# Diagonal tiles of a causal mask packed by 64 keys, masks as products, and a hinted last branch, in an attention kernel bound by its exponentials

**Chip, cores, metric.** One core of one Trainium2 chip. The metric is the time of one execution in device microseconds (us), median of several runs. A program on one core gives one time per run, and every comparison is made with runs of the kernel before on the same chip.

## The reference, cut to what matters

Two independent attention blocks over 2048 rows of 1024, 32 heads of 32. A is plain attention; B has four segments of 512 rows, a causal mask inside each segment and a memory that is carried from one segment to the next.

```python
# A
qkv = (x @ wqkv) ...                            # 32 heads of 32
p = softmax(einsum('bhqd,bhkd->bhqk', q, k) * Dh ** -0.5)
a = einsum('bhqk,bhkd->bhqd', p, v) ... @ wo
# B, for each of 4 segments of L = 512
mask = (ar[:, None] < ar[None, :]) * -1e9       # keys after the query are dead
p = softmax(einsum('bhqd,bhkd->bhqk', qs, ks) * scale + mask)
a_dot = einsum('bhqk,bhkd->bhqd', p, vs)
o = g * a_mem + (1 - g) * a_dot                 # a_mem from the carried memory M, z
M, z = M + phi(ks)^T vs, z + sum(phi(ks))
```

## The kernel before

The kernel is written as many small processes (projections, score batches, exponentials, values, outputs) that ask for buffers and engines. A scheduler at build time, with a cost for every instruction, turns them into one fixed list of instructions for each engine. So every instruction's place in its engine's queue is decided before the kernel runs.

Scores lie transposed in PSUM: keys on the partitions, queries on the columns, one bank of 512 columns for each of four heads, two banks to a pair, three pairs. ScalarE reads a pair (1024 columns), takes the exponential and writes the tile PT in SBUF. TensorE then multiplies PT with the values, and VectorE (DVE) copies the sums out of PSUM; such a copy, which frees a bank, is called an evacuation below. One batch of A is 512 columns for four heads, so two exponentials. B's batches for one unit (a segment and four heads):

```python
def parts(self, u, k):          # (key tile, first query, width, column in the bank)
    ...                         # A cut
    return [[(0, 0, 512, 0)], [(1, 128, 384, 0), (3, 384, 128, 384)], [(2, 256, 256, 0)]][k]

def s_batch(self, u, k):        # cut: waits for data, slots of PT
    one = u[0] == "B" and k == 2
    npair = 1 if one else 2
    prs = yield acq(self.pairs, npair)          # PSUM pairs
    ...
    yield do("PE", lambda e: f(e, mms), r=keys, w=w, cost=N256, prio=0, mode=ROW)
    for x in range(npair):
        Q.spawn(self.exps(u, k, x, prs[x], slots[x], one))

def exps(self, u, k, x, pr, sl, one):           # cut
    yield do("ACT", lambda e: e.activation(ap, self.ps[:, pr[0]:pr[1] + 1, :], ACTF.Exp, scale=sc),
             r=[("ps", bk) for bk in pr], w=keys, cost=0.9035, prio=0)
    Q.give(self.pairs, [pr])
    if u[0] == "B":                             # which 128 x 128 pieces hold a diagonal
        if k == 2:
            ms = [(bass.AP(..., ap=[list(ap.ap[0]), [256, 4], [1, P]]), 4)]
        else:
            ms = [(ap[:, :, c:c + P], 2) for c in ((0,), (0, 384))[k]]
        for m, n in ms:
            yield do("POOL", lambda e, m=m, n=n: e.affine_select(m, m, pattern=[[0, n], [1, P]],
                     compare_op=ALU.is_ge, fill=0.0, base=0, channel_multiplier=-1), ...)
```

At the end a flag says whether a slow fallback program must run; every engine reads it and branches:

```python
def f(eng):
    self.R.play(eng, name)
    self.R.after(eng, self.flagop)
    v = eng.value_load(self.flag[0:1, 0:1])
    with eng.If(v != 0):
        ...                                     # the fallback: a large second program
    if name == "SP":
        self.R.drain(eng)                       # last transfers landed
```

## Time and profile before

| | before |
|---|---|
| time, median (3 runs) | 1113.5 us (1112.8 to 1113.8) |
| span of the profiled run | 1111.6 us |
| first exponential starts, last one ends | 10.37, 1100.42 us |
| spacing of two exponentials (end to end), median | 917 ns |
| stalls between exponentials after 60 us | 2.3 us |
| end of the span after the last output's issue | 5.14 us |

"Stalls" is a sum that is used all through: for each exponential the time from the end of the one before it to its own end, less 917 ns (490 for one of 512 columns), added up over all that start after 60 us. It says how much time ScalarE lost in the body, whatever it waited for.

ScalarE (ACT) is the bound; the prediction below shows the lines. Its waits, in this view "engine, tile, line, what it waited for: us in total, times, longest":

```profile
ACT WoB L1002 <- PE ps L973: 7.3, 2, 6.6
ACT outsb L1202 <- PE ps L1197: 4.2, 3, 2.4
ACT PT L1002 <- PE ps L973: 2.5, 6, 0.7
```

The first row is the start of the program, the second its end. In between only the third is left: 2.5 us for scores. The chain of work that ended last, as shares of the span:

```profile
ACT 90%; PE 6%; DVE 2%; DMA 1%; POOL 1%; issue 0%
```

### The profile page before, as it was taken

The page shows a single profiled execution, that of the slowest core. Times are in us where ns is not written, and L with a number is a line of the kernel's source. Part 1 is how long each engine was busy: PE and PEld are TensorE (multiplying, and loading weights), DVE is VectorE, ACT ScalarE, POOL GpSimd, SP SyncE. Part 2 cuts the span into 40 slices and gives each one's busy share as a digit, 9 for nine tenths or more (in the row PEclk, how much of TensorE's full clock was granted, in tenths as well). Part 3 has the DMA queues.
Part 4 walks back from the last instruction along what each step waited for, and adds up shares of the span by engine and source line. Part 5 has one row for each costly group of instructions (what it writes and reads, how often), then busy time and mean ns, then how long its engine had stood idle before and what let it go on. Part 6 is the DMA issues. An engine that isn't in the chain of part 4 may idle for free.

```text
span 1111.6 us, 52489 instructions
## 1 busy us (share of the span) xinstructions
PE 1043.3 (94%) x24445; PEld 539.9 (49%) x24445; DVE 725.5 (65%) x1472; ACT 1089.7 (98%) x1189; POOL 136.8 (12%) x287
## 2 busy tenths in 40 slices
PE   8999999999899999989999999899999999999997
PEld 4545445454454444444455454444544444455454
DVE  2356556545675888888676788777566677664333
ACT  6999999999999999999999999999999999999996
POOL 1011111100201212121110301201111111110000
PEclk9999999999999999999999999999999999999999
DMA  9543332252122222142212232241132222201111
GB/s 186 103 104 86 64 69 46 50 93 55 31 50 41 55 64 60 43 85 52 58 46 55 45 60 65 50 84 40 41 55 50 45 45 60 88 18 36 41 41 66
DMA packets 213763, 67.40 MB, mean 61 GB/s; under 512 B 202786, under 2 KB 210978, under 8 KB 213538
## 3 DMA queue, kind: packets, MB, share of 16 engines
q1 hardware_dynamic: 212066, 63.07, 26.7%
q8 instruction: 192, 3.15, 1.3%
q10 hardware_dynamic: 1472, 0.92, 0.3%
q14 instruction: 33, 0.27, 0.1%
HBM read 36.70 MB, written 8.39 MB: 41 GB/s over the span
## 4 chain that ended last, share of the span: by engine, by line
ACT 90%; PE 6%; DVE 2%; DMA 1%; POOL 1%; issue 0%
ACT PT L1002 89%; PE ps L688 2%; PE ps L1109 2%; PE ps L1197 1%; PE ps L973 1%; DMA PKt<-PH 1%; ACT OTA L1002 1%; POOL PT L1011 0%; DMA OTA<-in_A_x_dram 0%; ACT OTB L1002 0%; DVE xA L625 0%; DVE VT L693 0%; PE ps L1244 0%; DVE PH L831 0%; DVE PH L1039 0%
## 5 line engine op out<-in xcount | busy, mean ns | idle before, releaser
L1002 ACT ACTIVATE PT<-ps 128x1024 bf16<-128x1024 f32 x1164 | 1068.2, 1265 | 2.7 <-PE ps L973 2.5
L1109 PE MATMUL ps<-PT,ones 128*32 128x256 bf16 (+1 forms) x4784 | 283.6, 270 | 1.2 <-issue 1.2
L1109 PE MATMUL ps<-PT,VA 128*32 128x256 bf16 x4016 | 241.3, 274 | 6.1 <-ACT PT L1002 5.0
L973 PE MATMUL ps<-QA,KA 32*128 32x256 bf16 x4096 | 203.4, 273 | 30.7 <-ACT PT L1002 25.5
L688 PE MATMUL ps<-xB,WB 128*32 128x512 bf16 (+1 forms) x3332 | 205.3, 364 | 2.4 <-DVE OD L1150 0.7
L1011 POOL TENSOR_SCALAR_AFFINE_SELECT PT<-PT 128x256 bf16<-128x256 bf16 (+1 forms) x224 | 106.5, 483 | 814.2 <-ACT PT L1002 808.9
L688 PE MATMUL ps<-xA,WA 128*32 128x512 bf16 (+1 forms) x3476 | 205.2, 356 | 1.3 <-DVE xA L625 0.6
L973 PEld LDWEIGHTS ps<-QA,KA 32*128 32x128 bf16 x4096 | 61.1, 92 | 193.6 <-ACT PT L1002 184.9
L1109 PEld LDWEIGHTS ps<-PT,ones 128*32 128x32 bf16 x4784 | 128.0, 97 | 32.8 <-issue 16.5
L1109 PEld LDWEIGHTS ps<-PT,VA 128*32 128x32 bf16 x4016 | 107.1, 96 | 44.8 <-issue 17.1
L688 PEld LDWEIGHTS ps<-xA,WA 128*32 128x32 bf16 x3476 | 80.4, 96 | 78.6 <-issue 28.0
L1150 DVE COPY OD<-ps 128x512 f32<-128x512 f32 x127 | 86.7, 682 | 43.7 <-PE ps L1109 42.7
L688 PEld LDWEIGHTS ps<-xB,WB 128*32 128x32 bf16 x3332 | 77.3, 96 | 77.7 <-issue 31.3
L1202 DVE CAST outsb<-ps 128x512 bf16<-128x512 f32 x55 | 37.9, 689 | 73.7 <-PE ps L1197 73.7
L693 DVE CAST VT<-ps 128x512 bf16<-128x512 f32 x64 | 44.1, 689 | 61.4 <-PE ps L688 57.5
L693 DVE CAST KQB<-ps 128x512 bf16<-128x512 f32 x64 | 44.1, 689 | 60.2 <-PE ps L688 60.2
L1197 PE MATMUL ps<-WoB,OTB 128*32 128x512 bf16 (+1 forms) x1100 | 68.2, 366 | 0.6 <-DVE OD L1150 0.6
L1156 DVE STREAM_TRANSPOSE OD<-Rall 128x256 f32<-128x256 f32 x127 | 56.0, 441 | 3.2
L1153 DVE STREAM_TRANSPOSE Dt<-OD 128x256 f32<-128x256 f32 x127 | 55.5, 437 | 2.9
L1197 PE MATMUL ps<-xA,OTA 128*32 128x512 bf16 (+1 forms) x888 | 53.4, 367 | 0.3 <-DVE KQB L693 0.3
L1109 PE MATMUL ps<-PT,VB 128*32 128x256 bf16 (+1 forms) x768 | 43.7, 257 | 7.4 <-POOL PT L1011 3.1
L973 PE MATMUL ps<-KQB 32*128 32x128 bf16 (+3 forms) x512 | 43.3, 302 | 6.6 <-ACT PT L1002 4.9
(95 smaller groups left out, 690.5 us busy)
## 6 DMA issues: line engine op xcount, KB each, us to landing
WB<-in_B_wk_dram SPq DMA_DIRECT2D x32, 256.0 KB, 3.0
WB<-in_B_wq_dram SPq DMA_DIRECT2D x32, 256.0 KB, 3.0
WB<-in_B_wv_dram SPq DMA_DIRECT2D x32, 256.0 KB, 3.2
out_dram<-outsb SPq DMA_DIRECT2D x63, 128.0 KB, 1.9
WA<-in_A_wqkv_dram SPq DMA_DIRECT2D x23, 256.0 KB, 3.2
WoB<-in_B_wo_dram SPq DMA_DIRECT2D x1, 2048.0 KB, 9.8
xA<-in_A_wo_dram SPq DMA_DIRECT2D x1, 2048.0 KB, 8.3
OTA<-in_A_x_dram SPq DMA_DIRECT2D x2, 256.0 KB, 5.5
```

The costliest lines, as they stand in the source:

```text
L688: ins = e.matmul(self.ps[32 * c:32 * c + 32, bank, lo:hi], W[:, i, 32 * c:32 * c + 32], x(i)[:, lo:hi], start=st, stop=sp)
L693: return e.tensor_copy(dst, self.ps[:, bank, 0:n])
L973: ins = e.matmul(self.ps[:, bk, col:col + w], lhs(t, hs), rhs(q0, w, hs), start=True, stop=True)
L1002: yield do("ACT", lambda e: e.activation(ap, self.ps[:, pr[0]:pr[1] + 1, :], ACTF.Exp, scale=sc), r=[("ps", bk) for bk in pr], w=keys, cos ...
L1011: yield do("POOL", lambda e, m=m, n=n: e.affine_select(m, m, pattern=[[0, n], [1, P]], compare_op=ALU.is_ge, fill=0.0, base=0, channel_mul ...
L1109: ins = e.matmul(out, l, r, start=st, stop=sp)
L1150: yield do("DVE", lambda e: e.tensor_copy(OD[:, :], self.ps[:, OB, :]), r=[("ps", OB)], w=[("OD", x), ("Rb", x)], cost=dve(2 * QU), prio=0 ...
L1153: yield do("DVE", lambda e: e.transpose(Dt[:, :], Rb), r=[("Rb", x)], w=[("Dt", x)], cost=dve(QU), prio=self.par["fp"], hold=0.15)
L1156: yield do("DVE", lambda e: e.transpose(Rb.rearrange("p (a b) -> p a b", b=32), self.spread(Rc)), r=[("Rc", ui % 64)], w=[("Rb", x)], cost ...
L1197: ins = e.matmul(self.ps[32 * c:32 * c + 32, bank, lo:hi], lhs(j)[:, 32 * c:32 * c + 32], W(j)[:, lo:hi], start=st, stop=sp)
L1202: return f(self.outsb[ob][:, :], self.ps[:, bank, :])
```

## The change

Its intent: of each 128 x 128 diagonal tile the quarter that is dead as a whole (upper 64 keys, lower 64 queries) is no longer computed. Two live 64-wide pieces of two tiles share 64 columns, one in the lower and one in the upper 64 partitions, by adding two products in PSUM, one of them with keys of which half are zero (KZ). The values do the same with half-zeroed values (VZ) and half-zeroed ones. A unit then needs 512 + 512 + 128 columns per head in place of 512 + 512 + 256, and the third exponential has 512 columns in place of 1024. As one short exponential leaves an odd half batch, batches are now made of two items each, which take two pairs together. The masks become products with a 0/1 tile, on POOL for the first batch and on DVE for the others. The branch at the end gets a hint (`branch_hint`), and the last waits come in order of issue. mR, a scratch tile for reading B's memory, now lies in the bytes of ze, the scratch of VectorE's other work, and has to be acquired like it. Constants of the scheduler were searched anew.

```diff
+HINT = {"PE": 99999, "ACT": 300, "DVE": 700, "POOL": 999, "SP": 999}   # operations before the end
-    par = dict(b=(16, 12, 9), mem=-4, ..., rate=0.58, ahead=20, sl=4, pv=10, ob=4, ..., slk=0.12, ...)
+    par = dict(b=(16, 12, 9), mem=-2, ..., rate=0.6, ahead=28, sl=7, pv=18, ob=1, ..., slk=0.3, ..., mk=(0, 1, 1), mp=0, ...)
 ...
-                self.R.play(eng, name)
+                loc = self.R.play(eng, name, HINT[name])
-                with eng.If(v != 0):
+                eng.br_eq(v, 0, on_true=over, on_false=again).branch_hint(loc)
+                with self.nc.body(again, valid_engines=[eng.engine]):
 ...
+    def b_k(self, n):       # half of each key tile, on POOL
+        yield do("POOL", lambda e: e.tensor_copy(self.KZ[:, :, 0:H], src), ..., cost=0.45, prio=1)
+    def b_v(self, n):       # halves of the values, on POOL
+        for j in range(2):
+            yield do("POOL", lambda e, j=j: e.tensor_copy(self.VZ[H * j:H * j + H, j:4:2, :], ...), ..., cost=0.52, prio=1)
 ...
-        return [[(0, 0, 512, 0)], [(1, 128, 384, 0), (3, 384, 128, 384)], [(2, 256, 256, 0)]][k]
+        H = P // 2
+        return [[("lo", 0, H, 0), ("hi", 1, H, 0), (0, H, 512 - H, H)], [(1, P + H, 5 * H, 0), (2, 2 * P + H, 3 * H, 5 * H)],
+                [("lo", 2, H, 0), ("hi", 3, H, 0), (3, 3 * P + H, H, H)]][k]
 ...
-        prs = yield acq(self.pairs, npair)
+        prs = yield acq(self.pairs, 2)
+        if one[0]:          # a short item first: three pieces on TensorE
+            ops = [(st[0][:3], banks[0], 0.1, None), (st[1], banks[1], N256, None), (st[0][3:], banks[0], 0.1, True)]
 ...
-            yield do("ACT", lambda e: e.activation(ap, self.ps[:, pr[0]:pr[1] + 1, :], ACTF.Exp, scale=sc),
-                     ..., cost=0.9035, prio=0)
+            n = 2 * P if one else 512
+            to = bass.AP(..., ap=[list(ap.ap[0]), [n, 2], [1, n]])
+            yield do("ACT", lambda e: e.activation(to, self.ps[:, pr[0]:pr[1] + 1, 0:n], ACTF.Exp, scale=sc),
+                     ..., cost=0.483 if one else 0.91, prio=0)
 ...
-                yield do("POOL", lambda e, m=m, n=n: e.affine_select(m, m, ...))
+            if self.par["mk"][k]:
+                yield do("DVE", lambda e: e.tensor_tensor(d, d, m, ALU.mult), ..., cost=dve(sz), prio=self.par["mp"])
+            else:
+                yield do("POOL", lambda e: e.tensor_tensor(d, d, m, ALU.mult), ..., cost=0.25 + sz * 0.0014, prio=0)
```

## The prediction

> **What bounds the kernel now.** I read the page's head and busy times first, then the groups of ScalarE (ACT) with shapes kept apart, then ACT's own waits.
>
> ```profile
> span 1111.6 us, 52489 instructions
> PE 1043.3 (94%) x24445; PEld 539.9 (49%) x24445; DVE 725.5 (65%) x1472; ACT 1089.7 (98%) x1189; POOL 136.8 (12%) x287
> ...
> L1002 ACT ACTIVATE PT<-ps 128x1024 bf16<-128x1024 f32 x1164 | 1068.2, 1265 | 2.7 <-PE ps L973 2.5
> L1002 ACT ACTIVATE WoB<-ps 128x1024 bf16<-128x1024 f32 x8 | 7.6, 1025 | 7.3 <-PE ps L973 7.3
> L1002 ACT ACTIVATE OTA<-ps 128x1024 bf16<-128x1024 f32 x8 | 7.6, 1048 | 0.0
> L1002 ACT ACTIVATE OTB<-ps 128x1024 bf16<-128x1024 f32 x4 | 3.8, 1105 | 0.0
> L1202 ACT CAST outsb<-ps 128x512 bf16<-128x512 f32 x3 | 1.8, 585 | 4.2 <-PE ps L1197 4.2
> ```
>
> The four ACTIVATE rows are all exponentials of the program: 1164 + 8 + 8 + 4 = 1184, each 128x1024. Their busy time is 1087.2 us of a span of 1111.6; of the 1164 in steady state only 2.7 us of idle time stand before them. So ACT is the bound, with no gaps to fill, and one exponential costs its spacing, 1087.2 / 1184 = 0.918 us. The mean of 1265 ns in the first row is not that cost: consecutive instructions overlap. The chain of waits says the same: ACT has 90% of it, and its longest piece is 570.38 us for 622 exponentials, 0.917 each.
>
> The code accounts for 1184. A has 8 head groups x 8 query blocks x 8 key batches x 2 = 1024. B has 32 units (4 segments x 8 head groups), each with five: two for the first batch, two for the second, one for the third: 160. Of these 5120 columns, a causal mask over 512 keys in tiles of 128 needs 4 heads x (512+384+256+128) = 5120. All are used, but half of each diagonal tile is thrown away afterwards.
>
> Outside ACT's solid stretch are a start (first exponential at 10.37 us) and a tail. I read the tail from the timeline and from the DMA view over one late microsecond:
>
> ```profile
> 1105.80 0.58 ACT L1202 CAST outsb<-ps 128x512 bf16<-128x512 f32 x1 [0.71 <-PE ps L1197]
> 1105.83 0.15 DVE L1302 CAST flag<-ps 32x1 int32<-32x1 f32 x1 [0.41 <-PE ps L1197]
> 1106.41 0.36 ACTq L1204 DMA_DIRECT2D out_dram<-outsb  x1
> ```
> ```profile
> q8 instruction: 1, 0.02, 10.2%
> q14 instruction: 1, 0.01, 1.9%
> ```
>
> The first block is the last work of any engine; the last output transfer lands about 1.9 us after its issue (median of that row on the page), near 1108.3. The flag that decides the branch is there at 1106.0. Yet the span ends at 1111.6. The second block is the stretch 1108 to 1109 us: one instruction block on each of two fetch queues and nothing else. Fetches also occur between 1107 and 1108 and after 1110. So the end, some 3.3 us after the last output, is about instructions being fetched behind the branch over the large fallback program, not about data.
>
> [...] (1025 - 585) / 512 = 0.86 ns per column between an exponential of 1024 and a cast of 512. [...]
>
> **The change part by part.**
>
> *Packing.* Each diagonal tile of 128x128 has only three of its four 64x64 blocks alive. The change puts the two live 64-key triangular pieces of two tiles on the same columns, one on the upper and one on the lower 64 partitions, by accumulating two products with half-zeroed keys. A unit then has 512 + 512 + 128 columns per head instead of 512 + 512 + 256: four exponentials of 1024 and one of 512. The count stays 1184, but 32 of them are halved. With 0.427 each this is 32 x 0.427 = 13.7 us; with the trace's 0.86 ns it would be 14.1. I take 13.7. It lies fully on the path, since ACT has no idle time to give back.
>
> *Masks.* 224 selects on POOL go (192 x 449 ns and 32 x 683 ns, 107 us). In their place come 64 products of 256 elements on POOL (first batch), and 64 of 256 plus 32 of 512 on DVE. The nearest DVE rows are tensor_tensor of 256 with f32 inputs, 415 to 454 ns, and 512 columns at 689; that gives at most 64 x 0.45 + 32 x 0.69 = 51 us. [...] I estimate 40: DVE goes from 725 to some 765 us, 70% of a shorter span. POOL: 64 products at 0.7 (estimate, above the 522 ns of its 128-wide product) are 45 us, and 96 copies of half keys and half values at 0.45 are 43. With the rest that stays, POOL is near 120 us, 11%. Nothing of this is on the path.
>
> *TensorE.* The streamed columns do not change: scores 576 + 512 + 192 = 1280 per head and unit, as before; values 384 + 896 = 1280, as before. There are more and shorter matmuls: 32 instead of 16 for scores and 80 instead of 48 for values and sums, 48 x 32 = 1536 more. In the timeline four 256-wide ones start every 0.108 us, 0.027 per 64 columns. If a pack of 64 columns takes twice its share, about 20 packs a unit lose 0.027 x 20 x 32 = 17 us. TensorE's idle time is 68 us, and it also spends 18.7 us on fillers that multiply by zero. So it stays beside ACT, at 95 to 96%.
>
> *Branch hint and order of the last waits.* [...] I take 2.0 us off (estimate, between 0 and the 3.3 us that stand there). Waiting for transfers in order of issue is a small part of it.
>
> *Retuned schedule.* Queue priorities, B's rate of 0.60 for 0.58 and margins move work of engines that are not the bound; I give it nothing in the middle.
>
> *New handoffs.* Before, a batch that needed one PSUM pair could start while two exponentials lay ahead. Now every batch takes two of the three pairs, so it starts when the first exponential of the batch before has ended, and has one exponential of 0.918 us as cover. A normal score batch takes 0.40 us plus 0.2 us of start (the timeline shows 0.21 idle before it). A batch with the short item has three pieces on TensorE, the last waiting for the first, and comes near 0.8 to 1.1. I charge 32 x 0.03 = 1.0 us.
>
> Sum: 1113.5 - 13.7 - 2.0 + 1.0 = 1098.8 us, 1.3% less.
>
> **The rivals.** *Handoff of the short item*: if its scores come 0.2 us late each time, 32 x 0.2 = 6.4 us come back, and the time is about 1104. For it: the tight cover just worked out. Against: the program orders its instructions by a model with latencies, and scores have first priority. *DVE or POOL late with masks*: a product waits for its exponential in a queue in fixed order and holds up evacuations behind it; value products then start late and the buffers of exponentials fill. DVE has stretches of 79% (157.76 of 200 us between 300 and 500). Against: 14 pairs of buffers, some 12 us of ACT work. If it bites it costs 2 to 5 us, about 1102. *TensorE becomes the bound*: only if short packs cost several times my estimate; then the 13.7 us would be eaten, near 1108. Unlikely with over 80 us of slack. *The hint does nothing[...]*: 1101[...]. *The end shrinks more*: with 3 us from the branch, 1.5 from the retuned tail and no handoff loss it is about 1095.
>
> **Range and chances.** Packing has an arithmetic ceiling of 14 us. To be faster by over 2% the time must be below 1091.2: 8 us more than I see, which only a much shorter tail could give. Slower by 2% (over 1135.8) would need a stall that the priorities should prevent. So 1094 to 1104, with 0.05 / 0.94 / 0.01.
>
> **What would show it.** ACT: 1152 exponentials of 128x1024 and 32 of 128x512, sum near 1073.5 us, spacing still 0.918. Idle time of ACT before exponentials between 20 us and the last one: 2 to 5 us; over 8 means that the handoff rival holds, with scores named as releaser. DVE near 765 us, POOL near 120, TensorE's idle time down to 40 to 60. From the last output's issue to the end of the span: 5.2 us before, near 3.2 after. It would be wrong if a 512-wide exponential cost much over 0.49 us, or if the first exponential or the tail moved by several us.

The 0.427 us that an exponential of half the columns takes less is what the profile after shows, 917 less 490 ns; the 2.0 us for the hint are an estimate, out of the 3.3 us read from the trace. That this end is about fetching was a reading of the transfers seen there. The 40 us of products on VectorE (DVE), no term of the sum, came to 35.0.

## The result, and the profile after

| | before | after | after, run again later (e14) |
|---|---|---|---|
| time, median us | 1113.14 (4 runs) | 1106.51 (4 runs, 1105.0 to 1109.2) | 1104.98 (5 runs) |
| ratio to before [95%] | | 0.9943 [0.9922, 0.9965] | 0.9921 [0.9908, 0.9934] |
| span of the profiled run | 1111.6 | 1105.4 | 1102.8 |
| first exponential starts | 10.37 | 11.36 | 11.14 |
| last exponential ends | 1100.42 | 1097.97 | 1095.32 |
| stalls after 60 us | 2.3 | 12.7 | 10.2 |
| last exponential to end of span | 11.13 | 7.42 | 7.43 |

A ratio is the mean time of one kernel's runs over that of the other's of the same rounds, so it is not quite the ratio of the medians quoted beside it.

The change is faster by 0.6 to 0.8%, where 1.3% was predicted, and the time lies outside the predicted range. The head of the page after:

```profile
span 1105.4 us, 54139 instructions
PE 1037.7 (94%) x25177; PEld 536.2 (49%) x25177; DVE 749.1 (68%) x1569; ACT 1078.7 (98%) x1188; POOL 123.0 (11%) x231
```

ScalarE is still busy 98% of the span, which looks like a kernel with nothing lost. Its groups by form tell more:

```profile
L1097 ACT ACTIVATE PT<-ps 128x1024 bf16<-128x1024 f32 x1132 | 1047.0, 1161 | 9.6 <-PE ps L1066 9.0
L1097 ACT ACTIVATE PT<-ps 128x512 bf16<-128x512 f32 x32 | 23.2, 725 | 0.0
```

The rows give busy us and mean ns of one, then the idle time in front and its releaser. The 32 short exponentials are there. In the trace each ends 490 ns after the one before it (median), a long one 917 ns: packing took 32 x 0.427 = 13.7 us of work away. But 9.6 us of idle time now stand before the long ones, where it was 2.7. ScalarE's waits after, to be held against the three rows shown of before:

```profile
ACT PT L1097 <- PE ps L1066: 9.0, 19, 1.4
ACT WoB L1097 <- PE ps L1066: 8.4, 2, 7.7
ACT outsb L1306 <- PE ps L1301: 3.3, 1, 3.3
```

Waits for scores came from 6 to 19 times and from 2.5 to 9.0 us. The chain agrees:

```profile
ACT 64%; PE 24%; DVE 7%; DMA 3%; issue 1%; POOL 0%; SPq 0%; DVEq 0%; POOLq 0%
```

Before, one engine carried nine tenths of the path. Now TensorE and VectorE carry a third of it between them, in pieces.

In one sum, from the two profiled runs: packing -13.7; stalls in the body 12.7 - 2.3 = +10.4; the first exponential 1.0 later, the first 60 us 0.2 better; the end 11.13 - 7.42 = -3.7. That is -6.2, the difference of the spans. With the later run of the same kernel, the stalls are +7.9 and the spans differ by 8.8. (The trace of the first has a stretch of 6.8 us at 127 us in which TensorE's granted clock was 0.5, right where 2 us of its stalls stand; that of the later run has none in the body. Such stretches of 3.4 or 6.8 us stand in the body of 14 of the 20 profiles here: not in that of before, but in two of its order, e1 and e9. Most places vary; in five of the nine profiles of the changed order one of 6.8 us stands at 126 to 129 us.) So between 8 and 10 of the 13.7 us that packing saved were lost again as stalls in the middle.

The masks themselves did what was expected of them. By form, with busy us, mean ns of one, and the idle time of the engine in front:

```profile
L1109 POOL TENSOR_TENSOR PT<-PT,mask 128x256 bf16<-128x256 bf16 x64 | 45.8, 715 | 352.1 <-ACT PT L1097 350.6
```
```profile
L1107 DVE TENSOR_TENSOR PT<-PT,mask 128x256 bf16<-128x256 bf16 x64 | 20.2, 316 | 7.8 <-ACT PT L1097 7.1
L1107 DVE TENSOR_TENSOR PT<-PT,mask 128x512 bf16<-128x512 bf16 x32 | 14.8, 463 | 10.9 <-ACT PT L1097 10.6
```

DVE has 35.0 us of products; POOL has 45.8, and 42.7 of the two kinds of copies (64 of 443 ns, 32 of 447), where 107.4 us of selects stood before.

What one stall looks like, in the timeline after. First TensorE, where a row is start, length, engine, line, operation, how many, and in brackets the idle time in front of it:

```profile
565.27 0.40 PE L1066 MATMUL ps<-QA,KA 32*128 32x256 bf16 x8
566.27 0.29 PE L1212 MATMUL ps<-PT,VB 128*32 128x256 bf16 x4 [0.60 <-DVE OD L1254]
...
566.91 1.90 PE L1301 MATMUL ps<-WoB,OTB 128*32 128x512 bf16 x32
568.74 0.40 PE L1066 MATMUL ps<-QA,KA 32*128 32x256 bf16 x8
```

and ScalarE over the same time:

```profile
564.80 3.00 ACT L1097 ACTIVATE PT<-ps 128x1024 bf16<-128x1024 f32 x3
569.19 2.85 ACT L1097 ACTIVATE PT<-ps 128x1024 bf16<-128x1024 f32 x3 [1.39 <-PE ps L1066]
```

Values of B (L1212) wait 0.60 us until VectorE has emptied a PSUM bank, then 32 matmuls of an output projection (L1301) take 1.90 us, and only then, 3.5 us after the last ones, come scores (L1066). ScalarE has exponentials in hand until 567.80 and then stands still for 1.39. The view says "waits for TensorE", and TensorE was busy nearly the whole time, with something else that stood first in its queue.

The end, last rows of the timeline after:

```profile
1102.37 0.39 ACTq L1308 DMA_DIRECT2D out_dram<-outsb  x1
1102.40 0.46 SPq L1360 DMA_DIRECT2D out_dram<-outsb  x1
1102.46 0.14 DVE L1406 CAST flag<-ps 32x1 int32<-32x1 f32 x1 [0.27 <-PE ps L1404]
```

From the flag's end (1102.61) to the end of the span it is 2.79 us, against 5.58 before. In the trace TensorE's compare-and-branch takes 0.40 us, before 4.61.

### The profile page after: what moved, and what is told of

Same layout as the page of the kernel before. It is cut to its first block, busy times and chain, and to the rows that moved or that the text cites. A ratio compares the mean times of both kernels' runs of the same rounds, so it can differ in the third digit from the quotient of the medians.

```text
span 1105.4 us, 54139 instructions
## 1 busy us (share of the span) xinstructions
PE 1037.7 (94%) x25177; PEld 536.2 (49%) x25177; DVE 749.1 (68%) x1569; ACT 1078.7 (98%) x1188; POOL 123.0 (11%) x231
## 4 chain that ended last, share of the span: by engine, by line
ACT 64%; PE 24%; DVE 7%; DMA 3%; issue 1%; POOL 0%; SPq 0%; DVEq 0%; POOLq 0%
ACT PT L1097 63%; PE ps L717 9%; PE ps L1212 6%; PE ps L1066 5%; PE ps L1301 3%; DMA VB<-VT 2%; PE ps L1348 1%; DMA VA<-VT 1%; DVE we L1133 1%; DVE VT L722 1%; DMA WA<-in_A_wqkv_dram 1%; DVE we L1134 1%; ACT OTA L1097 1%; DVE ze L1132 0%; DVE OD L1254 0%
## 5 line engine op out<-in xcount | busy, mean ns | idle before, releaser
L1212 PE MATMUL ps<-PT,ones 128*32 128x256 bf16 (+2 forms) x4784 | 283.8, 268 | 0.0
L1212 PE MATMUL ps<-PT,VA 128*32 128x256 bf16 x4016 | 241.9, 274 | 3.0 <-DVE OD L1254 0.8
L1066 PE MATMUL ps<-QA,KA 32*128 32x256 bf16 x4096 | 210.3, 274 | 33.5 <-ACT PT L1097 28.1
L717 PE MATMUL ps<-xB,WB 128*32 128x512 bf16 x3072 | 204.1, 381 | 4.2 <-DVE amem L913 1.0
L1066 PEld LDWEIGHTS ps<-QA,KA 32*128 32x128 bf16 x4096 | 62.8, 92 | 206.6 <-ACT PT L1097 190.8
L1212 PEld LDWEIGHTS ps<-PT,ones 128*32 128x32 bf16 x4784 | 128.1, 97 | 29.4 <-issue 13.2
L1212 PEld LDWEIGHTS ps<-PT,VA 128*32 128x32 bf16 x4016 | 107.1, 96 | 43.4 <-issue 24.0
L717 PEld LDWEIGHTS ps<-xB,WB 128*32 128x32 bf16 x3072 | 70.8, 96 | 76.7 <-issue 31.9
L1109 POOL TENSOR_TENSOR PT<-PT,mask 128x256 bf16<-128x256 bf16 x64 | 45.8, 715 | 352.1 <-ACT PT L1097 350.6
L853 POOL COPY VZ<-VB 64x256 bf16<-64x256 bf16 x64 | 28.4, 443 | 347.1 <-DMA VB<-VT 324.8
L1301 PE MATMUL ps<-WoB,OTB 128*32 128x512 bf16 x1024 | 66.3, 381 | 0.7 <-DVE OD L1254 0.6
L1212 PE MATMUL ps<-PT,VB 128*32 128x192 bf16 (+2 forms) x768 | 45.4, 243 | 8.8 <-DVE OD L1254 3.2
L1301 PE MATMUL ps<-xA,OTA 128*32 128x512 bf16 x832 | 53.2, 381 | 0.2 <-DVE outsb L1306 0.2
```

Of the source, the lines that this page charges most:

```text
L717: ins = e.matmul(self.ps[32 * c:32 * c + 32, bank, lo:hi], W[:, i, 32 * c:32 * c + 32], x(i)[:, lo:hi], start=st, stop=sp)
L853: yield do("POOL", lambda e, j=j: e.tensor_copy(self.VZ[H * j:H * j + H, j:4:2, :], V[0:H, j:4:2, 0:P]), r=[("VB", n % 2)], w=["VZ"], cost ...
L1066: ins = e.matmul(out, l, r, start=a, stop=z)
L1109: yield do("POOL", lambda e: e.tensor_tensor(d, d, m, ALU.mult), r=keys + ["mask"], w=keys, cost=0.25 + sz * 0.0014, prio=0)
L1212: ins = e.matmul(out, l, r, start=st, stop=sp)
L1301: ins = e.matmul(self.ps[32 * c:32 * c + 32, bank, lo:hi], lhs(j)[:, 32 * c:32 * c + 32], W(j)[:, lo:hi], start=st, stop=sp)
```

## The experiments

Eighteen kernels ran, in five lots; each lot has its own runs of the kernel before (medians 1113.98, 1113.92, 1113.9, 1114.45, 1113.69). Some give a wrong result, by touching fewer columns; their instruction order is then that of the kernel they come from, line for line, because the scheduler is still told the old cost. The check of results passed all of them but e11 and e18, so that passing does not tell that nothing was left out. Letters in the quoted expectations stand for theories and are explained where they stand; beware that S means in e5 and e6 that packing itself makes the scores late in any order, and in e16 that the old order can use a ScalarE that is shortened evenly. Where a cut inserts a line, line numbers behind it are higher by one or two.

### The branch

**e1** is the kernel before with the hint and the new order of last waits alone (the HINT, play, drain and emit parts of the diff above).

> The kernel before with only the branch hint and the new order of the last waits; its schedule and its packing of B are untouched. My theory: the two small parts shorten only the end, so the time falls by 2 to 3.5 us (1109.5 to 1111), ACT's exponentials keep their 917 ns spacing and its idle time, and the stretch from the last output's issue to the end of the span shrinks from 5.2 us to about 2.6. Rival 1 (the hint does nothing here, the shorter tail of after comes from its schedule): 1113, end stretch still 5.2. Rival 2 (a hint standing from the first instruction of TensorE [...] makes it late): TensorE idles more for no named reason and the time rises above 1114.

Measured: 1114.33, ratio 1.0001 [0.9984, 1.0017]. Nothing. From flag to end 5.56 us, and TensorE's branch still took 4.60 us. The other engines' branches take 0.04 to 0.08 us with the hint and without.

**e2** is the changed kernel with exactly these parts undone.

> The changed kernel without the hint and with the old order of the last waits: packing, masks and schedule as changed. My theory: it loses the 2 to 3.5 us at the end (1108.5 to 1110) and keeps all of ACT's stalls in the middle, about 10 us above spacing. Rival (the hint [...] makes TensorE's scores late): ACT's stalls shrink to 3 to 5 us and the time falls to 1103 or less.

Measured: 1107.21, ratio 0.9947 [0.9923, 0.9971]. From flag to end 5.59 us, TensorE's branch 4.41 us. So in the changed kernel the hint is worth 5.59 - 2.79 = 2.8 us at the end; in the kernel before the same hint is worth nothing, because it fails on TensorE. The whole times show it less clearly: e2 lies under its expected range, 0.7 us above the changed kernel's first runs (the ratios differ by 0.0004) and 2.9 us above e14 by ratios.

**e15** moves TensorE's hint in the kernel before from its first instruction to 300 operations before its end.

```diff
-HINT = {"PE": 99999, ...}
+HINT = {"PE": 300, ...}
```

> The kernel before with the branch hint, but TensorE's hint stands 300 operations before its end and not at its first instruction, where it missed (its branch took 4602 ns there, 397 ns in the changed kernel with the same hint). If the place of the hint decides, the branch takes about 0.4 us and the stretch from the flag to the end of the span falls from 5.6 to about 2.8 us, the time to 1110.5 to 1111.5. If not, the branch takes 4.6 us again and the time stays at 1113 to 1114.5.

Measured: 1113.25, ratio 0.9988 [0.9975, 1.0002]; branch 4.57 us, flag to end 5.53. So the hint did nothing in either place tried, at the first instruction (4.60 us, e1) or here. In the nine profiles without a working hint TensorE's branch takes 3.6 to 5.3 us; where the hint works it takes 0.40 (after, e14, e12; 0.49 in e5). Why TensorE's hint works in the changed kernel and not in the one before stays open.

### Masks, copies, amount of TensorE work

**e3**: the mask products of the changed kernel touch one column each (wrong).

```diff
+            d, m = [bass.AP(tensor=t.tensor, offset=t.offset, ap=[list(t.ap[0]), [1, 1]]) for t in (d, m)]
```

> The changed kernel, same instruction order on every engine, but each mask product covers one column only (the result is wrong on purpose). It takes away some 25 to 30 us of DVE time and some 25 us of POOL time. Theory M (the masks on DVE and POOL hold up evacuations and value products, which makes the scores late): ACT's excess over its spacing falls from about 12 us to 6 or less and the time falls by 5 us or more, to 1101. Theory O (the instruction order with a shorter ACT leaves TensorE too little slack, masks only add a little): the time falls by less than 3 us.

Measured: 1103.75, ratio 0.991 [0.9893, 0.9926]; stalls 9.5. Against e2 it is 3.5 us faster, and 2.8 of these are the hint that e2 lacks. Against e14 by ratios it is 1.2 us. The masks cost one microsecond or so, not the ten.

**e10**: as e3, and the copies of half keys and half values move one element.

```diff
-... self.KZ[:, :, 0:H], src) ...            -... self.VZ[H * j:H * j + H, j:4:2, :], V[0:H, j:4:2, 0:P]) ...
+... self.KZ[:, 0:1, 0:1], src[:, 0:1, 0:1]) +... self.VZ[H * j:H * j + H, j:j + 1, 0:1], V[0:H, j:j + 1, 0:1])
```

> The changed kernel, same instruction order, with masks of one column and with the copies of half keys and half values on POOL cut to one element (wrong on purpose). The thin masks alone gave 1103.8. If the copies on POOL are a further cause (scores wait for half keys, value products for half values), the time falls by another 1.5 us or more, to 1102 or less; if not, it stays at 1103 to 1104.5.

Measured: 1104.11, ratio 0.99 [0.9884, 0.9915]; stalls 10.9. No further gain that the intervals could show.

**e11**: the output projections of the changed kernel stream half of their columns (wrong).

```diff
+            hi = (lo + hi) // 2
```

> The changed kernel, same instruction order, but most products of the output projections use half of their columns (wrong on purpose): TensorE has some 45 to 50 us less work. Theory G (TensorE has too little slack behind a shorter ACT): ACT's excess in the middle falls from 12.7 + 2.3 us to 7 or less and the time falls to 1097 to 1100 (up to 1.5 us of it in the tail). Theory W (waits of TensorE's queue for other engines and transfers make the stalls, not its amount of work): the excess stays above 10 us and the time at 1104 or more.

Measured: 1102.44, ratio 0.9902 [0.9884, 0.992]. Some 2 us of gain against e14's ratio. In its profile the stall shown above shrank from 1.5 to 0.3 us as excess over the spacing (with 0.6 at the next), as that projection now takes 1.05 us:

```profile
564.07 1.05 PE L1302 MATMUL ps<-WoB,OTB 128*32 128x256 bf16 x32
565.05 0.40 PE L1066 MATMUL ps<-QA,KA 32*128 32x256 bf16 x8
```
```profile
565.50 1.94 ACT L1097 ACTIVATE PT<-ps 128x1024 bf16<-128x1024 f32 x2 [0.16 <-PE ps L1066]
```

Stalls altogether are still 10.8 us, but 4.3 of them, 1.5 at one exponential and 2.8 at two others, stand beside half-clock stretches. Without these three exponentials 6.5 us are left, where e14 has 9.5. So neither theory holds as it was written: the amount of work in the output projections explains some 3 us of the stalls.

**e18** takes the other projections, those of the inputs: of their eight accumulated steps the seven later ones stream half of their columns. (The expectation speaks of each projection; the edit leaves the output projections as they were.)

```diff
+            hi = hi if st else (lo + hi) // 2
```

> The changed kernel, same order and number of instructions; in each projection of 8 accumulated steps the seven later ones stream only half of the columns (wrong on purpose). TensorE's busy time falls by some 160 to 180 us, nearly everywhere in the body. Theory T (stalls come because TensorE has too much to do around them): stalls between exponentials after 60 us fall from 10.4 to 4 us or less, 1098 to 1100. Theory W (they come from waits of the order itself, handoffs and evacuations, whatever the amount): 8 us or more stay, 1102 to 1105.

Measured: 1103.96, ratio 0.9901 [0.9886, 0.9917]. TensorE's busy time fell from 1037.7 to 920.2 us (I had expected 160 to 180 us off, it was 117), and the stalls stayed: 11.0 us, a part of them beside five half-clock stretches. At the 39 exponentials whose stalls recur in three profiles of this order (below) 8.4 us are left of 10.6 in e14; at three of the 39 they are 1.2 us longer than in e14, beside half-clock stretches. The same stall as above, on TensorE and on ScalarE:

```profile
561.89 0.29 PE L1213 MATMUL ps<-PT,VB 128*32 128x256 bf16 x4 [0.60 <-DVE OD L1255]
...
562.53 1.90 PE L1302 MATMUL ps<-WoB,OTB 128*32 128x512 bf16 x32
564.37 0.40 PE L1067 MATMUL ps<-QA,KA 32*128 32x256 bf16 x8
```
```profile
558.61 4.81 ACT L1098 ACTIVATE PT<-ps 128x1024 bf16<-128x1024 f32 x5
564.82 1.94 ACT L1098 ACTIVATE PT<-ps 128x1024 bf16<-128x1024 f32 x2 [1.39 <-PE ps L1067]
```

Over 100 us of TensorE's work are gone and this gap is 1.39 us, as it was, because the output projection in front of these scores still takes 1.90 us; e11, which halved that one, all but closed the gap. By time and stalls theory W of that expectation holds: less work elsewhere in TensorE takes only 2 to 3 us of stalls away. In the stall shown it is not how busy TensorE is in all that counts, but what stands in its queue right in front of the scores.

### Is it the order? The same kernel again

**e14** is the changed kernel unaltered.

> The changed kernel once more, to set its time beside the others of this job and to see what part of ACT's stalls recurs: I expect 1105 to 1108, an excess in the middle of 10 to 13 us, and the same large stalls (about 150, 332, 570, 602 and 1030 us) in the same places, because they belong to the order; those of the clock dips may move.

Measured: 1104.98, ratio 0.9921 [0.9908, 0.9934]; stalls 10.2. Put the three profiles of this order side by side (after, e2, e14), exponential by exponential:

| number of the spacing, from 0 | near, us | after | e2 | e14 |
|---|---|---|---|---|
| 219 | 216 | 303 ns | 303 | 303 |
| 345 | 332 | 820 | 823 | 822 |
| 409 | 390 | 473 | 473 | 469 |
| 471 | 447 | 419 | 418 | 415 |
| 605 | 570 | 1495 | 1493 | 1494 |
| 639 | 602 | 765 | 766 | 759 |
| 697 | 655 | 480 | 483 | 479 |
| 1109 | 1031 | 619 | 621 | 618 |

Excess over the spacing at eight of them, chosen because they recur, equal within 7 ns in each case. Adding up for every exponential the smallest of the three excesses, where it is over 20 ns (39 of them), gives 10.1 us, of 10.2 to 12.7 in all. So nearly all of it is built into the fixed order; chance adds up to 2.5 us in a run. The scheduler's own model of this order, from which the kernel is built, has 10.4 us of gaps between exponentials after 60 us, the largest at the same places, and 0.04 us for the kernel before: the change's schedule accepted them.

### Can the order before use a shorter ScalarE?

**e9**: the kernel before, its 32 third exponentials of B cut to half of their columns, nothing else (wrong). This is packing's saving without packing's order.

```diff
-            yield do("ACT", lambda e: e.activation(ap, self.ps[:, pr[0]:pr[1] + 1, :], ACTF.Exp, scale=sc),
+            yield do("ACT", lambda e: e.activation(ap[:, :, 0:256] if one else ap, self.ps[:, pr[0]:pr[1] + 1, 0:256 if one else 512], ACTF.Exp, scale=sc),
```

> The kernel before with nothing of the change, same instruction order, but each of its 32 exponentials for B's third batch reads and writes only half of its columns (wrong on purpose). ACT loses the same 13.7 us as in the change, without new masks, copies, matmuls, pairing or schedule. Theory P (the packing's own new dependencies and its order make the stalls; the old order could use a shorter ACT): the time falls by 11 to 14 us, to 1100 to 1103. Theory G (whatever shortens ACT, TensorE and the others behind it cannot follow, because they have no more slack): the time falls by only 4 to 8 us, to 1106 to 1110, and ACT's excess in the middle rises from 2 to 5 us to about 10.

Measured: 1107.37, ratio 0.994 [0.9926, 0.9955]: 6.5 us gained of 13.7. Of the stalls, 8.0 us, 5.5 stand at the exponential right behind a short one, 0.17 us each. ScalarE is done 0.43 us earlier and the next scores are not. That is my handoff rival, in the old order. The time lies in theory G's range; whether G's reason holds, that the others cannot follow however ScalarE is shortened, is what e16 tests.

**e13** was to shorten every exponential a little instead. By a slip (a variable that is used again further down in the same function) it cut B's 160 exponentials to 4 or 8 columns, and only A's to 505 of 512:

> The kernel before, same instruction order, with ACT's work shortened by nearly as much as packing does, but spread: some 1150 of the 1184 exponentials leave out 14 of their 1024 columns (1150 x 14 x 0.833 ns = 13.4 us; wrong on purpose). No pair of exponentials becomes tight, as the one after a short one does. Theory H (the old order and the engines behind it can follow a shorter ACT; what the run with halved exponentials lost, it lost at the handoff after each short one): the time falls by 12 to 13.5 us, to about 1101. Theory G (TensorE and the rest cannot follow a shorter ACT at all): it falls by 6 to 8 us, to about 1107, and ACT's stalls before scores appear in many places.

(The 0.833 ns a column in it is what the profile after shows: 917 - 490 = 427 ns for 512 columns.)

```profile
L1004 ACT ACTIVATE PT<-ps 128x1010 bf16<-128x1010 f32 x990 | 902.4, 1121 | 45.6 <-PE ps L973 45.2
L1004 ACT ACTIVATE PT<-ps 128x4 bf16<-128x4 f32 x128 | 20.6, 256 | 41.1 <-PE ps L973 41.1
...
L1004 ACT ACTIVATE PT<-ps 128x8 bf16<-128x8 f32 x32 | 5.7, 178 | 31.4 <-PE ps L973 31.4
```

Measured: 1095.41, ratio 0.9841 [0.9827, 0.9855]. As the test it was meant to be it is void. It shows another thing: ScalarE's busy time is 954.1 us, 136 less than before, and the kernel is only 18.5 us faster; the last exponential ends at 1080.5 instead of 1100.4. With B's exponentials next to free, that is all that the old order gives: some 20 us in reserve, not the "over 80 us of slack" that the prediction read from TensorE's busy time. It is not the limit of the other engines alone, since A's exponentials still hold 31% of the chain that ended last; no run freed these too.

**e16** is what e13 should have been.

```diff
+            nc = 505 if all(s in self.filled for s in sl) else 512
+            self.filled |= set(sl)
-            yield do("ACT", lambda e: e.activation(ap, self.ps[:, pr[0]:pr[1] + 1, :], ACTF.Exp, scale=sc),
+            yield do("ACT", lambda e: e.activation(ap[:, :, 0:nc], self.ps[:, pr[0]:pr[1] + 1, 0:nc], ACTF.Exp, scale=sc),
```

> The kernel before, same order. What e13 was meant to be: every exponential of steady state reads 505 of its 512 columns of each bank (wrong on purpose). e13 by a slip cut the 160 exponentials of B to 2 or 4 columns, some 140 us of ScalarE work, and came to 1095.4 all the same; so it measured a floor of about 1095 that TensorE sets in the old order. Here ScalarE loses 1164 x 12 ns = 13.7 us (905 against 917 ns, measured in e13), spread evenly. Theory S (the old order can use a shorter ScalarE as long as it is not shortened in lumps): 1100 to 1102, stalls between exponentials after 60 us under 4 us. Theory T (TensorE is so near its floor that only part can be used wherever it is saved): 1104 to 1107, stalls 5 to 8 us.

Measured: 1102.81, ratio 0.9897 [0.9882, 0.9912], so 10.9 us of some 13.7, and the waits for scores hardly grew:

```profile
ACT PT L1004 <- PE ps L973: 3.9, 6, 1.5
```

Six waits as before; the longest, 1.5 us, follows on a projection for which TensorE waited 1.8 us for a transfer of inputs (xB). The run falls between the theories, nearer to S: the time is 0.8 us above S's range, where the end of the span was 0.9 us longer than in the kernel before, and the stalls against a spacing of 905 ns are 4.9 us, where S allowed 4. The same 13.7 us, taken evenly, come through to four fifths; taken in lumps of 0.43 us, to half (e9).

### How fast is the new order without ScalarE?

**e17** cuts B's exponentials to 4 columns in the changed kernel, as e13 did in the old one.

```diff
+            nx = 2 if u[0] == "B" and all(s in self.filled for s in sl) else n
-            to = bass.AP(..., ap=[list(ap.ap[0]), [n, 2], [1, n]])
-            yield do("ACT", lambda e: e.activation(to, self.ps[:, pr[0]:pr[1] + 1, 0:n], ACTF.Exp, scale=sc),
+            to = bass.AP(..., ap=[list(ap.ap[0]), [n, 2], [1, nx]])
+            yield do("ACT", lambda e: e.activation(to, self.ps[:, pr[0]:pr[1] + 1, 0:nx], ACTF.Exp, scale=sc),
```

> The changed kernel, same order, B's 160 exponentials cut to 4 columns each (wrong on purpose), as e13 did by a slip in the old order; ScalarE loses some 125 us. The floor that TensorE's own order sets. Its tail is some 3.7 us shorter than the old kernel's, so with the same floor in the body: 1091 to 1093 (theory T: the change ran into a floor that was there before). If the new order raised TensorE's floor: 1096 or more. If TensorE had the slack of over 80 us that the prediction gave it: under 1060.

Measured: 1101.71, ratio 0.9889 [0.9874, 0.9904]. ScalarE's busy time is 965.5 us, 113 below that of the changed kernel, and only 3 to 5 us come of it. The last exponential ends at 1093.2. Beside e13's 1080.5:

| last exponential ends, us | as built | with B's exponentials next to free | difference |
|---|---|---|---|
| kernel before | 1100.4 | 1080.5 (e13) | 19.9 |
| changed kernel | 1095.3 (e14) | 1093.2 (e17) | 2.1 |

So the change took 13.7 us from ScalarE and also made the pace of the rest slower, by up to 12.7 us. Not all of this is the order's: e13 also shortened A's exponentials by 12 ns each, which e17 does not. In e13's chain A's exponentials have 31% of the span (32% in e17's), some 374 exponentials of 905 ns; 12 ns each are 4.5 us. My estimate is therefore that the old order had 15 us in reserve and that the new one's pace is 8 us slower. TensorE's own work is only 4.5 us of it at most (1036.6 us busy in e17, 1032.1 in e13). The expectation for a floor that the change raised ("1096 or more") is met, the one for a common floor (1091 to 1093) is not.

### Giving ScalarE's time back

**e4**: the changed kernel, but the 32 short exponentials go over their 512 columns twice; same order.

```diff
+            src = self.ps[:, pr[0]:pr[1] + 1, 0:n]
+            if one:
+                to = bass.AP(..., ap=[list(ap.ap[0]), [512, 2], [n, 2], [1, n]])
+                src = bass.AP(..., ap=[list(src.ap[0]), [0, 2], [512, 2], [1, n]])
```

> The changed kernel, same instruction order, but each of the 32 short exponentials does its 512 columns twice, so ACT gets back the 13.7 us that packing took. If ACT were the bound with fixed stalls, the time would rise by 13.7 us to 1120. Theory O (stalls are there because ACT now runs ahead of TensorE and DVE, which eat part of the gain): stalls shrink as ACT gets slower and the time rises by only 6 to 10 us, to 1113 to 1116.5.

Measured: 1116.45, ratio 1.0029 [1.0012, 1.0045]; stalls 7.7, none behind the wide ones. Giving 13.7 us back costs 10 to 12 us (against 1106.5, and against e14 by ratios). So in the new order most of a microsecond given back to ScalarE shows in the time, although e17 says that next to nothing more could be taken. The change sits at the point where ScalarE and the rest are equally fast: taking 13.7 us brought 10 to 12 there, and the order that goes with it lost most of these again against the old one.

### Other orders

The scheduler of the change is told 0.910 and 0.483 us for exponentials that take 0.917 and 0.490. **e5** tells it the measured ones, lets POOL do the third batch's masks too, and has its constants searched anew.

```diff
-    par = dict(..., rate=0.6, sl=7, pv=18, ob=1, bpos=16, fs=0.15, pvw=3, slk=0.3, pat=0.0, mk=(0, 1, 1), mp=0, ...)
+    par = dict(..., rate=0.59, sl=5, pv=14, ob=2, bpos=12, fs=0.1, pvw=2, slk=0.08, pat=0.1, mk=(0, 1, 0), mp=-1, ...)
-                     ..., cost=0.483 if one else 0.91, prio=0)
+                     ..., cost=0.490 if one else 0.917, prio=0)
```

> The changed kernel with the same packing and hint, but its scheduler told the durations of exponentials that the trace shows (0.917 and 0.490 us in place of 0.910 and 0.483), its constants searched anew for the shortest modelled schedule (in which ACT then idles some 1 us in the middle), and the masks of the third batch on POOL as well (the search chose that). Theory O (the gain is lost to an instruction order with gaps before the scores, which nothing in the packing forces): ACT's excess over its spacing after the first 60 us falls from about 12.7 + 2.3 us to 5 or less and the time falls to 1097 to 1101. Theory S (packing itself, by its handoffs, masks and short matmuls, makes the scores late in any order): the excess stays above 10 us and the time stays at 1104 to 1108.

**e6**: the same with the masks where the change has them and POOL's products told as 0.36 us plus 1.4 ns a column, and with constants from a search of its own (od, fp and td differ too).

> As the run before it, but with the masks on the same engines as in the change (first batch on POOL, second and third on DVE), and the scheduler told also the 0.715 us of a POOL product; another search, whose model keeps about 2.5 us of gaps in the middle. Theory O: 1098 to 1102, ACT's excess in the middle 4 to 7 us. Theory S: 1104 to 1108. If only the run before it is fast, the masks' place on DVE is the cause (theory M).

**e7**, the control: the kernel before, told 0.917 for 0.9035, constants searched anew in the same way.

> Control: the kernel before, no packing and no hint, with the same treatment: its scheduler told 0.917 us for an exponential and its constants searched anew. In the middle it has only 2.3 us of excess to lose, so theory O expects 1110 to 1114 (a little from a shorter tail at most). If it fell below 1106, the gain of the two runs before would be one of searching and not of packing.

**e8**: e6 without the hint.

> The second run of this job without the branch hint and with the old order of the last waits; the order of instructions is the same. If the hint is worth what the trace shows at the end (TensorE's branch 397 ns instead of about 4400 to 4600, the stretch from the flag to the end of the span 2.8 instead of 5.6 us), this one is 2.8 us slower than that run. Rival: the body gets that much slower with the hint (the pair changed kernel and its copy without the hint had equal times), and the two are within 1 us.

| | median us | ratio [95%] | stalls after 60 us | of these behind short ones | in the first 60 us |
|---|---|---|---|---|---|
| e5 | 1104.82 | 0.9913 [0.99, 0.9926] | 11.1 | 0.0 | 5.0 |
| e6 | 1105.93 | 0.9927 [0.9913, 0.994] | 10.1 | 0.3 | 4.2 |
| e7 | 1114.3 | 1.0001 [0.9988, 1.0014] | 7.0 | | 1.0 |
| e8 | 1108.62 | 0.9955 [0.9939, 0.9972] | 9.3 | 0.3 | 3.5 |

(Stalls are those of the profiled run, which in e5 and e7 was the slowest of its five.) The stalls behind short exponentials, 2.3 us in the changed kernel, go away when the scheduler knows the durations. The rest does not: other stalls take their place, some of them at the start. The scheduler's model has 1.1 us of gaps for e5 and 2.5 for e6, so these are not gaps that the search accepted. Times and stalls meet what theory S of e5 and e6 said (1104 to 1108, over 10 us), so it is not excluded that packing costs this in any order. e7 shows that true durations alone gain nothing in the old kernel, e8 that the hint is worth 1108.62 - 1105.93 = 2.7 us here too.

**e12** was chosen in the scheduler's model for orders that stand late transfers well: each candidate's fixed order was replayed with random extra time on its transfers.

```diff
-    par = dict(b=(16, 12, 9), ..., rate=0.6, sl=7, pv=18, ob=1, lead=6, bpos=16, wob=60, od=8, fp=2, fil=0.65, slk=0.3, pat=0.0, mk=(0, 1, 1), mp=0, ...)
+    par = dict(b=(14, 10, 7), ..., rate=0.59, sl=5, pv=14, ob=2, lead=5, bpos=12, wob=50, od=6, fp=3, fil=0.6, slk=0.08, pat=0.2, mk=(0, 1, 0), mp=1, ...)
```
(and the costs as in e6)

> A version meant to beat both: packing and hint as in the change, masks of the third batch on POOL, the scheduler told the measured durations of ACT and POOL, its constants chosen for the order that, replayed engine by engine with measured durations and with transfers that land late at random, keeps ACT idle least. Such a replay gave 17 us of idle in the middle for the changed kernel (measured 15), 10 for the first re-searched run (11) and 9 for the second (10), 4 for the kernel before (2 to 5) and gives 3 us for this one. If the order is what costs, the excess in the middle is 3 to 6 us and the time 1097 to 1101; if late landings and clock dips decide, it stays at 1103 to 1106.

Measured: 1102.65, ratio 0.9896 [0.988, 0.9913]; correct, none of its stalls behind a short exponential. It is the fastest version that leaves nothing out, 1.0% under the kernel before, about 3 us under the changed one by the ratio of e14. The time lies between the two ranges expected. Its profile still has 10.7 us of stalls, where the model has 0.7 and the replay had promised 3, but of another kind. The largest, on TensorE:

```profile
98.24 0.20 PE L1213 MATMUL ps<-PT,VB 128*32 128x64 bf16 x2
101.32 0.21 PE L1213 MATMUL ps<-PT,VB 128*32 128x64 bf16 x2 [2.88 <-issue]
```

These are the two halves of one group of four matmuls with the same operands ready, and 2.88 us between them in which TensorE waited for no semaphore. In these 3 us the DMA engines were busy 98% of the time, and one block of instructions was among what they moved:

```profile
q1 hardware_dynamic: 542, 1.09, 95.7%
q8 instruction: 1, 0.02, 2.1%
```

Pauses of 1 us or more without a named reason, in TensorE's weight loads or in its matmuls, stand in most of the profiles and come back at the same instructions of an order: near 47 us in all six profiles of the old order (1.45 us in that of before) and near 440 us in six of the nine of the changed one. Just before or in those looked up (before, e14, e12) a block of instructions was moved; in that of before it had been moved by 46.5 us, TensorE paused until 47.97, and hardly any transfer ran meanwhile (0.1% of the DMA engines). That the blocks cause the pauses is not shown.

A second kind is VectorE beside POOL's larger products:

```profile
851.29 2.86 POOL L1110 TENSOR_TENSOR PT<-PT,mask 128x256 bf16<-128x256 bf16 x3 [13.03 <-ACT PT L1098]
...
852.35 1.27 DVE L1133 TENSOR_SCALAR ze<-ze 128x512 int32<-128x512 int32 x1
853.54 1.15 DVE L1134 SCALAR_TENSOR_TENSOR we<-ue 128x512 f32<-128x512 f32 x1
```

The same two instructions of VectorE take 0.44 and 0.72 us on average in the changed kernel. Here, beside POOL's products, they took 0.83 and 0.43 us more; why, the trace does not show. Added up over the changed kernel, what VectorE's instructions take over the median of their form, where it is over 100 ns, is 7.9 us (4.7 before), 6.1 of it while a mask product ran on POOL; e3 bounds what comes of it on the path.

## Why the prediction was wrong, step by step

**The bound, and packing: right.** 1184 exponentials, 32 of them halved, 490 against 917 ns: 13.7 us, to the tenth. "It lies fully on the path, since ACT has no idle time to give back" is where the argument has its hole. ScalarE had no idle time at its old pace, for which the order kept scores ready. Take time from it, and what counts is how far the others are behind.

**The step that failed**: "Retuned schedule ... I give it nothing in the middle", with "New handoffs ... I charge 32 x 0.03 = 1.0 us". That term is 7.9 us in the undisturbed profile and 10.4 in the first one. 2.3 us of it stand directly behind the short exponentials, 0.07 each where I took 0.03. The rest stands elsewhere, at places fixed by the order (10.1 us recur in three profiles); in the stall shown a value group waits for an evacuation and an output projection stands before the scores. The rival that I named for a loss in the middle, the short item's handoff (0.2 us each, 6.4 us), came near in its result, 1104, by luck, as it was mostly wrong in its place; it is what would have happened in the *old* order (e9: 0.17 each, 5.5 us).

**TensorE beside ScalarE: the working was nearly right and the conclusion wrong.** Packs of 64 columns start every 0.03 us, as short as I could hope, and TensorE's busy time even fell by 5.6 us. "Unlikely with over 80 us of slack" took idle time as reserve. e13 shows that in the old order freeing B's exponentials gains 20 us (15 by my estimate without A's shortening), and e17 that in the new one it gains 2. Here idle time that lay inside the waits of a fixed order could not be spent.

**Masks: right, nearly.** DVE 749 against 765 predicted (35 us of products against 40), POOL 123 against 120, about 1 us on the path (e3) where I took nothing. The median products on DVE took 293 ns (256 columns) and 424 (512); the means, 316 and 463, are higher through some long ones, of 534 and 894 ns at most. The rival "masks late" falls.

**The end: right in kind, too small.** -2.8 us from the hint where I took 2.0 (5.59 to 2.79 between e2 and after), and 0.9 us more from what stands before the flag in the new order. I inferred it from the blocks of instructions that are moved behind the branch: in the trace of before seven of these, and nothing else, are moved after 1108 us. That the branch waits for them is not shown; what the traces show is TensorE's branch, 4.41 us in e2 and 0.40 in after. e1 and e15 show that I could as well have got nothing: with the hint the branch of the kernel before still took 4.60 and 4.57 us.

**The sum.** In spans the prediction is 1111.6 - 14.7 = 1096.9, the profiled run was 1105.4: +9.4 for stalls beyond the 1.0 charged, +1.0 for the later first exponential, -0.2 in the first 60 us, -1.7 for the end: +8.5. The test I had set, "over 8 means that the handoff rival holds, with scores named as releaser", came out at 9.0 with scores named; it told that something was late, not what.

**What stays open.** Which part of the new order makes the rest slower, by an estimated 8 us: two pairs taken at once by every batch, the longer chain of value pieces of B, the scratch mR that now shares memory with ze, or the constants. No experiment separates these, and that one of them undoes any order's reserve (theory S of e5) is not excluded. The search for other orders removed the stalls behind short exponentials and got 3 us; an order with the old one's reserve was not found, so whether one exists is not known. And why TensorE's hint works in one program and not in the other.

## What to carry to other kernels

Before taking time from the engine that bounds a kernel, measure how far the others are behind: cut that engine's work to almost nothing in the same order (the result may be wrong) and see where the time stops. Here a run that freed a part of it, B's exponentials, said 20 us where TensorE's idle time said 68. And when a change comes with a new static order, hold the order to account separately: here the scheduler's own model had 10.4 us of gaps in the new order before anything ran, and of the stalls that recurred in three profiles (10.1 of 10.2 to 12.7 us, the eight listed within 7 ns) the largest stood at the same places. A model without gaps is no promise: e5, e6 and e12 have 0.7 to 2.5 us in it and stalled for 10 to 11.
